# One 512 KB transfer for the first four row tiles, and a new order for the first 200 places of a hand-kept task list

## The chip, the cores and the metric

The kernel runs on one core of one Trainium2 chip. Its time is the device time of one execution in microseconds (us). Three timed runs of the kernel before gave 194.25, 195.13 and 196.08 us; the median, 195.13 us, is what the changed kernel is compared with.

Five engines run side by side, each with its own queue that is worked off in order: PE (matrix products and transposes), DVE and ACT (element-wise work and copies out of PSUM, the memory that PE writes), POOL (small vector work) and SP (which here only issues transfers). An engine that comes to an instruction whose input is not ready waits, and everything behind it on that queue waits too.

## The reference

The input rows are normalized, and two branches run over them. Branch A is a gated long convolution: a four-tap convolution of k, times v, then a convolution over all 2048 positions by FFT, times the rows. Branch B is a gated feed-forward product. They are joined at the end.

```python
x = A_q                                        # 1 x 2048 x 512
xn = _layernorm(x)
k_shift = sum over t of k_pad[:, t:t+S] * shift_k[:, ks-1-t]     # 4 taps
kv = k_shift * v
y = irfft(rfft(kv, 2S) * rfft(ssm_k, 2S))[:S] + kv * ssm_D       # long convolution
s = xn * y
h = gelu(xn @ w_gate) * (xn @ w_up)            # 512 x 1792 weights
g = silu(h @ w_down)                           # 1792 x 512 weights
return x + s * g
```

## The kernel before, in words

The 2048 rows are 16 tiles X of 128 rows, worked in four groups q of four tiles. For each group: statistics of each tile on DVE (line 821 and 822, `ln`), the reciprocal root on POOL (831 and 832), the normalized tile XN on DVE (835), four PE transposes of each tile (854, `xn_transpose`), copied out of PSUM into xnT (609). Then come 14 units m (`unit`): gate and up products (called at line 1117 through 618) of xnT with a 128-column piece of Wg and Wu, gelu of the gate on ACT (1128 or 1137), the product with the up part on DVE (1130 or 1140) into HT. Units 0 and 1 of group 0 are cut into halves a and b of two row tiles each, so that half a needs only tiles 0 and 1. The weights lie in four chunks; chunk 0 serves units 0 and 1, chunk 1 units 2 to 5. Last in each group are the down products with Wd.

The long convolution is done as a two-stage transform by matrix products. Its filter ssm_k is loaded as Hn0 to Hn3 (512 KB each). Hn0 and Hn1 are transposed by PE as f32 pairs (878, `h_transpose`), copied to HTr, and multiplied by the table F1 (`half1`, called "filter halves" here; each is two 128x256 products). Filter half "6/0" is the one of HTr tile 6 and transpose block 0; block 0 comes from Hn0, block 1 from Hn1. HTr holds eight tiles; the transposes of one block come in two lots of four, one for tiles 0 to 3 and one for tiles 4 to 7.

Eleven products of zeros (`warm_up`) run on PE before any data is there.

What sets the order: the program first makes a list of tasks, numbered in the order in which they are added; each issues one or several instructions. `SEQ` names all of them in the order in which they are emitted, so it fixes the order on each engine's queue; a "b" behind a number puts a copy on DVE that would else be on ACT. Waits between engines follow from the data and the buffers. `Sched.run` walks through `SEQ` with estimated durations (`LOAD_NS`, `LANDS`, and so on); these estimates choose only which of several free buffers a task takes, above all which of the eight PSUM banks. All loads named in `ORDER` are issued from the SP queue, in the order that they have in `SEQ`: in the kernel before the first two tiles of X, Hn0, the next two tiles, Hn1, chunk 0 of Wg and Wu, X1 (tiles 4 to 7), chunk 1 of Wg, and so on.

Of the kernel before, what the change touches and what calls it, by code (L numbers as in the profile page):

```python
# [22 lines left out]
LAST = [(0, 384), (384, 512)]  # L23
TURN = 8192
N_WARM = 11
ORDER = "x02 h0 h1 x22 w0 w1 h2 h3 D0 w2 s0 k0 v0 x1 w3 k1 v1 d0 d1 k2 v2 k3 v3 x2 x3"
SEQ = (
# [22 lines left out]
)  # L50
NF_BANKS = 4
ISSUE = 470.0
LOAD_NS = {("x0_", 262144): 1400.0, ("x0_", 131072): 450.0, 262144: 900.0, 524288: 1350.0, ("x", 524288): 2100.0, ("h", 524288): 1300.0, ("wg", 524288): 1550.0, ("wu", 524288): 1450.0, 917504: 2620.0, ("sk", 524288): 1500.0, 344064: 1250.0, 46080: 350.0, 3072: 100.0, 1024: 200.0}
W_XT, W_SW, W_BK, W_BH, W_ZI, W_BI, W_ZK, W_MI, W_G1 = 1665000, 600000, 555000, 703000, 333000, 640000, 490000, 740000, 222000
NC_PAIRS = 4
SMALL = 1.15 * 262144
# [235 lines left out]
class Sched:  # L292
# [8 lines left out]
    FIRST = {"loads": 1050.0, "SP": 30500.0}  # L301
    DRAIN = 121.0
    EARLY, TAKEN, SHARED, WAIT = (0.0, 1.0), 1400.0, 46000.0, 3300.0
    LANDS = (4350.0, 5590.0, 7100.0, 8420.0, 9350.0, 10200.0, 11500.0)

    def __init__(self):
        self.tasks = []
# [37 lines left out]
    def run(self):  # L345
        free = dict(self.FIRST)
        pipe = 0.0
        n_loads = 0
        order = []
        pmode = 0  # L350
        for name in SEQ.split():
            t = self.tasks[int(name.rstrip("b"))]
            eng, dur = t.opts[name[-1] == "b"]
            base = 0.0
            for d in t.deps:
                base = max(base, d.end if eng == d.eng == "PE" else d.end + d.lat + (self.SEM if not d.nbytes or eng != "PE" else 400.0 if d.eng == "loads" else self.HEDGE))
            for b in t.w:
                if b.pool is not None and b.slot is None:
                    f, b.slot = b.pool.find()
                    b.pool.take(b.slot)  # L360
                    base = max(base, f + self.SEM)
            t.start, t.eng = max(base, free.get(eng, 800.0)), eng
            free[eng] = t.end = t.start + dur + (self.DRAIN if eng == "PE" and t.mode != pmode else 0.0)
            pmode = t.mode if eng == "PE" else pmode
            if eng == "loads":
                free[eng] = t.start + dur * (self.EARLY[1] if t.start < self.EARLY[0] else 1.0)
                if n_loads < len(self.LANDS):
                    free[eng] = self.LANDS[n_loads] - self.LOAD_LAT
                n_loads += 1
                t.end = free[eng] + self.LOAD_LAT  # L370
            elif t.nbytes:
                en = t.end
                if en < self.SHARED:
                    free["loads"] += self.TAKEN
                pipe = max(pipe, en + self.DMA_LAT / 2) + t.nbytes / (self.SHARE_BW if en < self.SHARED else self.DMA_BW)
                t.end = pipe + self.DMA_LAT / 2 + (self.WAIT if en < self.SHARED else 0.0)
            for b in set(t.r + t.w):
                b.left -= 1
                b.last_end = max(b.last_end, t.end + t.lat)
                if b.left == 0 and b.pool is not None:  # L380
                    b.pool.release(b.slot, b.last_end)
            order.append(t)
        assert sorted(t.n for t in order) == list(range(len(self.tasks)))
        return order
# [14 lines left out]
def build_kernel(nc, A_q, A_k, A_v, A_shift_k, A_ssm_k, A_ssm_D, B_w_gate, B_w_up, B_w_down, out):  # L399
    with ExitStack() as es0:  # L400
# [107 lines left out]
        def dsem(name):  # L508
            return DSem(nc.alloc_semaphore(name), name)
# [79 lines left out]
        def dma(eng, out_ap, in_ap, sem, r, w):  # L589
            trk.dma(eng, lambda e: e.dma_start(out=out_ap, in_=in_ap), sem, r=r, w=w)  # L590
# [3 lines left out]
        def load(name, out_ap, in_ap, w_res, w_buf, nbytes, ring="SP", r=(), rb=()):  # L594
            sem = dsem("d_" + name)
            ns = LOAD_NS.get((name.rstrip("0123456789"), nbytes)) or LOAD_NS[nbytes]
            last_load[0] = S.add([("loads", ns)], lambda e: dma(ring, out_ap, in_ap, sem, r, w_res), r=rb, w=w_buf, nbytes=nbytes)
# [211 lines left out]

        for what in ORDER.split():  # L810
            if what[0] in "xa" and len(what) == 3:
# [475 lines left out]
```

## Time and profile before

| | |
|---|---|
| three timed runs | 194.25, 195.13, 196.08 us |
| profiled execution, first to last instruction (span) | 193.3 us |
| median of the timed runs less this span | 1.8 us |
| PE busy | 188.6 us, 98% |
| DVE busy | 160.0 us, 83% |
| ACT busy | 125.4 us, 65% |
| granted TensorE clock, mean | 1.000 |

The page gives the span of the profiled execution, and no time of its own for what lies around it (start and finish); the difference of 1.8 us from the timed median stands for that.

In a timeline row the first number is the start in us, the second the length of the merged stretch, then the engine, the line, the operation, what it writes and reads, and how many instructions are merged. PE instructions overlap, so a stretch's length holds a tail that lies under the next row: the pace of PE is read from start to start. In a row of transfers the last number is the time from the issue to the landing.

### The profile page before, as it was taken

Reading aid. Unit: us, or ns where it says so; the run is one execution under the profiler, and the core shown is the slowest. Engines: PE = TensorE matmul, PEld = TensorE weight load, DVE = VectorE, ACT = ScalarE, POOL = GpSimd, SP = SyncE. Lnnn points to the kernel's source line nnn. Section 1 sums busy time; section 2 is a strip of 40 time slices with the busy share of each in tenths; the row PEclk is TensorE's granted clock in tenths of the full one; section 3 lists DMA queues with packets and bytes.
Section 4 is the critical chain, followed back from the end, with each engine's and each line's share of the span. In section 5 each row is a group of like instructions: output and inputs, shape, how many; then the busy total and the mean of one; then the engine's idle time right before and its main releaser. Section 6 shows DMA issues by size and latency. Waiting matters only on the chain.

```text
span 193.3 us, 3502 instructions
## 1 busy us (share of the span) xinstructions
PE 188.6 (98%) x1377; PEld 85.6 (44%) x1377; DVE 160.0 (83%) x245; ACT 125.4 (65%) x170; POOL 13.9 (7%) x32
## 2 busy tenths in 40 slices
PE   7899999999999999999999999999999999999993
PEld 2685544444444444443434433433444334444452
DVE  6699789998999995877888789878897863588993
ACT  6787999969885987868548766856577431232121
POOL 5412420000000000020300000000000000000000
PEclk9999999999999999999999999999999999999999
DMA  5999999999999679999999991984805345939333
GB/s 175 311 307 349 377 400 347 157 249 372 375 374 354 196 264 259 390 323 305 218 285 230 338 320 59 288 276 147 264 10 195 106 140 153 389 112 353 132 139 136
DMA packets 45958, 49.19 MB, mean 254 GB/s; under 512 B 12787, under 2 KB 39671, under 8 KB 45942
## 3 DMA queue, kind: packets, MB, share of 16 engines
q1 hardware_dynamic: 37366, 42.67, 70.1%
q10 hardware_dynamic: 8576, 6.29, 10.3%
q8 instruction: 11, 0.18, 0.4%
q14 instruction: 5, 0.04, 0.1%
HBM read 27.39 MB, written 14.68 MB: 218 GB/s over the span
## 4 chain that ended last, share of the span: by engine, by line
PE 93%; DMA 4%; SPq 1%; DVE 1%; ACT 0%; issue 0%
PE psall L618 86%; PE psall L1028 5%; DMA Hn<-in_A_ssm_k_dram 4%; PE psall L854 1%; SPq L590 1%; PE psall L878 1%; DVE G L1175 0%; DVE G L1174 0%; ACT G L1172 0%
## 5 line engine op out<-in xcount | busy, mean ns | idle before, releaser
L618 PE MATMUL psall<-xnT,Wu 128*128 128x512 bf16 (+1 forms) x232 | 55.8, 372 | 0.0
L618 PE MATMUL psall<-xnT,Wg 128*128 128x512 bf16 (+1 forms) x232 | 55.3, 372 | 0.0
L618 PE MATMUL psall<-Wd,HT 128*128 128x512 bf16 (+2 forms) x238 | 52.0, 367 | 0.0
L1140 DVE TENSOR_TENSOR HT<-psall,GE 128x512 bf16<-128x512 f32 x54 | 36.7, 685 | 15.8 <-PE psall L618 15.4
L1137 ACT ACTIVATE GE<-psall 128x512 bf16<-128x512 f32 x54 | 31.7, 601 | 13.1 <-PE psall L618 12.9
L618 PEld LDWEIGHTS psall<-Wd,HT 128*128 128x128 bf16 x238 | 22.4, 98 | 25.9 <-issue 1.1
L618 PEld LDWEIGHTS psall<-xnT,Wg 128*128 128x128 bf16 x232 | 21.9, 98 | 25.4 <-issue 1.3
L618 PEld LDWEIGHTS psall<-xnT,Wu 128*128 128x128 bf16 x232 | 21.6, 98 | 25.9 <-issue 3.5
L609 ACT ACTIVATE X<-psall 128x1024 bf16<-128x1024 f32 (+1 forms) x18 | 15.1, 843 | 3.3 <-DMA ZH<-X 1.9
L609 ACT ACTIVATE HS<-psall 128x1024 bf16<-128x1024 f32 x14 | 13.7, 1022 | 4.4 <-PE psall L1028 4.4
L1164 ACT ACTIVATE G<-psall 128x512 bf16<-128x512 f32 x12 | 7.0, 598 | 12.9 <-PE psall L618 12.4
L1011 DVE TENSOR_TENSOR KAC<-KAC,KTM 128x2048 bf16<-128x2048 bf16 x12 | 14.6, 1217 | 0.1
L1009 DVE TENSOR_TENSOR KTM<-KK,SKB 128x2048 bf16<-128x2048 bf16 x12 | 14.6, 1217 | 0.0
L609 ACT ACTIVATE BO<-psall 128x1024 bf16<-128x1024 f32 x9 | 9.1, 1022 | 8.2 <-PE psall L1028 7.7
L609 ACT ACTIVATE KB<-psall 128x1024 bf16<-128x1024 f32 x11 | 11.0, 1021 | 3.6 <-PE psall L1028 3.6
L609 ACT ACTIVATE AST<-psall 128x1024 bf16<-128x1024 f32 x12 | 12.4, 1033 | 0.7 <-PE psall L618 0.5
L612 DVE CAST BO<-psall 128x1024 bf16<-128x1024 f32 x7 | 8.5, 1224 | 3.7 <-PE psall L1028 3.7
L821 DVE BATCH_NORM_STATS2 stats<-X 128x6 f32<-128x512 bf16 x16 | 10.3, 675 | 1.1 <-DMA X<-in_A_q_dram 1.1
L1172 ACT ACTIVATE G<-psall 128x512 bf16<-128x512 f32 (+2 forms) x5 | 2.6, 512 | 13.1 <-PE psall L618 13.1
L1091 DVE TENSOR_TENSOR HW<-KB,HW 128x1024 bf16<-128x1024 bf16 x16 | 10.9, 682 | 0.0
L1091 DVE TENSOR_TENSOR HS<-KB,HS 128x1024 bf16<-128x1024 bf16 x16 | 10.8, 682 | 0.0
L1166 DVE SCALAR_TENSOR_TENSOR G<-G,psall 128x512 bf16<-128x512 bf16 x12 | 7.8, 680 | 2.0 <-ACT G L1164 2.0
(83 smaller groups left out, 175.6 us busy)
## 6 DMA issues: line engine op xcount, KB each, us to landing
BH<-ZH SPq DMA_DIRECT2D x8, 512.0 KB, 6.1
HW<-HS SPq DMA_DIRECT2D x16, 256.0 KB, 3.2
BK<-ZK SPq DMA_DIRECT2D x8, 512.0 KB, 5.1
ZI<-BO ACTq DMA_DIRECT2D x16, 256.0 KB, 2.8
BI<-ZI SPq DMA_DIRECT2D x8, 512.0 KB, 4.2
ZK<-AST SPq DMA_DIRECT2D x6, 512.0 KB, 4.1
Hn<-in_A_ssm_k_dram SPq DMA_DIRECT2D x4, 512.0 KB, 8.4
KK<-in_A_k_dram SPq DMA_DIRECT2D x4, 512.0 KB, 8.6
```

The source lines that it names most:

```text
L609: return h.activation(o, i, ACTF.Copy, scale=scale)
L612: return h.tensor_copy(o, i)
L618: return h.matmul(o, lhsT=l, rhs=r, start=st, stop=sp)
L821: t_stats[t] = op([("DVE", 670.0)], lambda e, h, t=t: h.bn_stats(stats[:, t, :], X[:, t, :]), r=[bX[q][t % 4]], w=[bst[t]], rr=[R_X[t]], w ...
L1009: op([("DVE", dur)], lambda e, h, j=j, m=m: h.tensor_tensor(KTM[:, m.slot, :, :], kk(j), sk(j), ALU.mult), r=need + [bSKB[j], a], w=[m], r ...
L1011: op([("DVE", dur)], lambda e, h, m=m: h.tensor_tensor(KAC[:, a.slot, :, :], KAC[:, a.slot, :, :], KTM[:, m.slot, :, :], ALU.add), r=[m], ...
L1028: trk.op("PE", lambda h: h.matmul(ps(s, i)[b, :], lhsT=wt(col)[a, :], rhs=data(col)[a, :], start=n < 16, stop=n >= len(todo) - 16, tile_po ...
L1091: return hd.tensor_tensor(o, flat(KB, kb[h]), o, ALU.mult)
L1137: op([("ACT", act(512))], lambda e, h: h.activation(GE[:, g.slot, :], bank(pg), ACTF.Gelu_apprx_tanh), r=[pg], w=[g], rr=lambda: R_bank(pg ...
L1140: op([("DVE", dve(512, 1))], lambda e, h: h.tensor_tensor(HT[:, q % 2, m, :], bank(pu), GE[:, g.slot, :], ALU.mult), r=[pu, g], w=[bHT[q][m]],
L1164: op([("ACT", act(n))], lambda e, h, g=g, pc=pc: h.activation(g, pc(), ACTF.Tanh, scale=0.5), r=[p], w=[bt], rr=lambda p=p: R_bank(p), ww= ...
L1166: op([("DVE", dve(512, 1))], lambda e, h, g=g, pc=pc: h.scalar_tensor_tensor(out=g, in0=g, scalar=1.0, in1=pc(), op0=ALU.add, op1=ALU.mult ...
```

## The change

The first four tiles of X come in one transfer of 512 KB (128 partitions of 4 KB) in place of two of 256 KB (2 KB per partition): `x04` stands in `ORDER` for `x02` and `x22`. There is one task fewer, so every number above 20 falls by one in the new `SEQ`. The first 200 places of `SEQ` are new; from there on both lists are the same but for that shift. The loads keep their order on the SP queue, the second piece of X left out. The planner's table of landing times counts bytes in place of loads.

Three copies change engine: xnT of tiles 0 and 1 goes from ACT to DVE, the second HTr lot of block 1 from DVE to ACT. On PE each of the first 53 tasks after the warm-up is the same in both lists, in another order; from the 54th on the two queues are equal. The first of them, by name (old numbers in brackets):

| | PE queue before | PE queue after |
|---|---|---|
| 1, 2 | Hn0 transposes, two lots (50, 49) | Hn0 transposes (49, 50) |
| 3, 4 | xn tile 0 (82), filter half 7/0 (117) | Hn1 transposes (54, 53) |
| 5, 6 | xn tile 1 (83), filter half 5/0 (107) | filter half 6/0 (112), xn tile 0 (82) |
| 7, 8 | filter half 6/0 (112), Hn1 transposes (54) | filter half 5/0 (107), xn tile 1 (83) |
| 9, 10 | Hn1 transposes (53), gate 0a (369) | filter half 4/0 (102), xn tile 2 (84) |
| 11, 12 | filter half 5/1 (109), xn tile 2 (84) | filter half 5/1 (109), xn tile 3 (85) |
| 13, 14 | up 0a (370), xn tile 3 (85) | up 1a (378), gate 1a (377) |
| 15, 16 | up 1a (378), gate 1a (377) | gate 0a (369), gate 0b (373) |
| 17, 18 | gate 0b (373), gate 1b (381) | gate 1b (381), up 0a (370) |
| 19 to 21 | up 0b (374), up 1b (382), filter half 7/1 (119) | **gate 3 (389)**, filter half 4/1, up 1b |
| 22 | **gate 3 (389)** | filter half 7/0 |

Gate 3 is the first product that needs chunk 1 of Wg.

On DVE the old order takes the statistics of tiles 0 and 1, then XN of tiles 0 and 1, then the same for 2 and 3. The new one takes all four statistics first, then XN 0, 1 and 2, the copy of xnT 0, XN 3, the copy of xnT 1. On ACT the first copies are, after: HTr of block 0 (52) and of block 1 (56), filter halves 5/0 and 4/0 (108, 103), xnT 2 and xnT 3 (88, 89); then the gelus.

```diff
-ORDER = "x02 h0 h1 x22 w0 w1 h2 h3 D0 w2 s0 k0 v0 x1 w3 k1 v1 d0 d1 k2 v2 k3 v3 x2 x3"
+ORDER = "x04 h0 h1 w0 w1 h2 h3 D0 w2 s0 k0 v0 x1 w3 k1 v1 d0 d1 k2 v2 k3 v3 x2 x3"
 SEQ = (
-    "17 18 0 3 1 2 4 8 5 7 11 20 6 9 50 12 65 66 67 73 19 68 75 74 49 10 76 13 52 21 82 22 86 117 83 69 107 70 71 112 54 72 87 77 56b 78 53 369 "
-    "51 108 36 79 371 109 84 88 80 370 15 85 372 23 31 89 110 378 377 113 27 373 379 381 383 375 14 453 455 457 380 24 458 374 459 25 454 118 382 "
...
+    "0 3 17 2 1 18 19 11 8 9 10 4 12 64 66 65 5 7 48 67 6 72 74 68 69 70 73 13 49 51 53 55 52 76 111 71 20 21 35 22 81 106 75 82 77 107 30 26 78 "
+    "23 85b 101 102 83 87 108 79 84 88 86b 377 376 378 14 458 454 24 456 368 379 372 370 380 374 369 371 388 112 109 31 27 29 382 50 459 452 32 "
...
 )
-LOAD_NS = {("x0_", 262144): 1400.0, ("x0_", 131072): 450.0, ...
+LOAD_NS = {("x0_", 524288): 1400.0, ("x0_", 131072): 450.0, ...
...
-    LANDS = (4350.0, 5590.0, 7100.0, 8420.0, 9350.0, 10200.0, 11500.0)
+    LANDS = ((0.0, 2650.0), (524288.0, 4050.0), (1048576.0, 5450.0), (1572864.0, 6850.0), (1835008.0, 7720.0), (2097152.0, 8590.0), (2621440.0, 10590.0), (3145728.0, 12390.0))
...
-        n_loads = 0
+        n_loads = 0.0
...
-                if n_loads < len(self.LANDS):
-                    free[eng] = self.LANDS[n_loads] - self.LOAD_LAT
-                n_loads += 1
+                n_loads += t.nbytes
+                for (b0, t0), (b1, t1) in zip(self.LANDS, self.LANDS[1:]):
+                    if b0 < n_loads <= b1:
+                        free[eng] = t0 + (t1 - t0) * (n_loads - b0) / (b1 - b0) - self.LOAD_LAT
```

More of the change, by code (lines that the diff above doesn't have):

```diff
@@ L52 @@
 ISSUE = 470.0
-LOAD_NS = {("x0_", 262144): 1400.0, ("x0_", 131072): 450.0, 262144: 900.0, 524288: 1350.0, ("x", 524288): 2100.0, ("h", 524288): 1300.0, ("wg", 524288): 1550.0, ("wu", 524288): 1450.0, 917504: 2620.0, ("sk", 524288): 1500.0, 344064: 1250.0, 46080: 350.0, 3072: 100.0, 1024: 200.0}
+LOAD_NS = {("x0_", 524288): 1400.0, ("x0_", 131072): 450.0, 262144: 900.0, 524288: 1350.0, ("x", 524288): 2100.0, ("h", 524288): 1300.0, ("wg", 524288): 1550.0, ("wu", 524288): 1450.0, 917504: 2620.0, ("sk", 524288): 1500.0, 344064: 1250.0, 46080: 350.0, 3072: 100.0, 1024: 200.0}
 W_XT, W_SW, W_BK, W_BH, W_ZI, W_BI, W_ZK, W_MI, W_G1 = 1665000, 600000, 555000, 703000, 333000, 640000, 490000, 740000, 222000
```

40 rows, old and new, of the table SEQ are left out of this document.

## The prediction

> **What bounds the kernel now.** I read the page first (span and chain by engine), then the chain of waits in order of time, then the waits of PE alone, then the timeline of PE over the first 15 us.
>
> ```profile
> span 193.3 us, 3502 instructions
> PE 93%; DMA 4%; SPq 1%; DVE 1%; ACT 0%; issue 0%
> ```
>
> ```profile
> 2.12 7.16 DMA Hn<-in_A_ssm_k_dram
> ...
> 30.27 51.16 PE psall L618 x238
> ...
> 189.55 0.02 issue
> ```
>
> The chain leaves the loads at 9.3 us and is PE until 189.55. That alone doesn't say that PE never waits in between; its own waits from 6 to 189 us do (waiter, what was waited for, total, times, longest):
>
> ```profile
> PE psall L878 <- DMA Hn<-in_A_ssm_k_dram: 0.5, 1, 0.5
> PE psall L618 <- ACT HTr L609: 0.2, 1, 0.2
> ```
>
> Both fall into the first 11 us; the same question from 11 us on has an empty answer. So PE has a fixed amount of work, and the end moves by just as much as the idle time of PE changes. The change reorders PE's work and adds none. In 51.16 us the chain holds 238 products, 0.215 us each: PE's full pace. All that can be won is what PE lost in this stretch:
>
> ```profile
> 0.97 4.87 PE L618 MATMUL psall<-AST 128*128 128x512 bf16 x11 [0.97 <-DVE AST L671]
> 5.64 1.71 PE L878 MATMUL psall<-ident,Hn 128*128 128x128 f32 x8
> 7.18 0.39 PE L854 MATMUL psall<-ident,XN 128*128 128x128 bf16 x4
> 7.82 0.39 PE L618 MATMUL psall<-HTr,F 128*128 128x256 bf16 x2 [0.25 <-ACT HTr L609]
> 8.04 0.39 PE L854 MATMUL psall<-ident,XN 128*128 128x128 bf16 x4
> 8.27 0.60 PE L618 MATMUL psall<-HTr,F 128*128 128x256 bf16 x4
> 9.32 1.16 PE L878 MATMUL psall<-ident,Hn 128*128 128x128 f32 x8 [0.46 <-DMA Hn<-in_A_ssm_k_dram]
> 10.32 0.60 PE L618 MATMUL psall<-xnT,Wg 128*128 128x256 bf16 x4
> 10.82 0.39 PE L618 MATMUL psall<-HTr,F 128*128 128x256 bf16 x2
> 11.23 0.38 PE L854 MATMUL psall<-ident,XN 128*128 128x128 bf16 x4
> 11.45 0.60 PE L618 MATMUL psall<-xnT,Wu 128*128 128x256 bf16 x4
> ...
> 14.96 0.59 PE L618 MATMUL psall<-xnT,Wg 128*128 128x512 bf16 x2
> ```
>
> Prices, from start to start: two 128x256 products 7.82 to 8.04, 0.22, so four are 0.44; four bf16 transposes 11.23 to 11.45, 0.22; eight f32 transposes 9.32 to 10.32, 1.00 (0.125 each), but 5.64 to 7.18, 1.54 (0.19 each) the first time. The warm-up ran at 4.67 us for eleven, 0.42 each against 0.215 later: the transposes at 7.18 are as long (0.39) as their like at 8.04, so until about 7.0 PE works at half pace, though the mean granted clock in the table above is 1.000. Gaps: 7.18 + 0.22 = 7.40 to 7.82, 0.42; 8.27 + 0.44 = 8.71 to 9.32, 0.61; 10.32 + 0.44 = 10.76 to 10.82, 0.06; 10.82 + 0.22 = 11.04 to 11.23, 0.19. Together 1.28 us; with the 0.5 us that half pace costs the first transposes, 1.8 us is the most that this change could win.
>
> **Part one: the transfers.** Issues on the SP queue, and each one's time to landing:
>
> ```profile
> 0.72 0.40 SPq L590 DMA_DIRECT2D X<-in_A_q_dram  x1
> 1.18 0.42 SPq L590 DMA_DIRECT2D Hn<-in_A_ssm_k_dram  x1
> 1.64 0.43 SPq L590 DMA_DIRECT2D X<-in_A_q_dram  x1
> 2.12 0.44 SPq L590 DMA_DIRECT2D Hn<-in_A_ssm_k_dram  x1
> 3.08 0.70 SPq L590 DMA_DIRECT2D Wu<-in_B_w_up_dram  x1
> 3.83 0.55 SPq L590 DMA_DIRECT2D X<-in_A_q_dram  x1
> 4.42 0.64 SPq L590 DMA_DIRECT2D Wg<-in_B_w_gate_dram  x1
> ```
>
> ```profile
> X<-in_A_q_dram SPq DMA_DIRECT2D x1, 256.0 KB, 3.3
> Hn<-in_A_ssm_k_dram SPq DMA_DIRECT2D x1, 512.0 KB, 4.2
> X<-in_A_q_dram SPq DMA_DIRECT2D x1, 256.0 KB, 6.3
> Hn<-in_A_ssm_k_dram SPq DMA_DIRECT2D x1, 512.0 KB, 7.2
> Wu<-in_B_w_up_dram SPq DMA_DIRECT2D x1, 256.0 KB, 7.9
> X<-in_A_q_dram SPq DMA_DIRECT2D x1, 512.0 KB, 8.6
> Wg<-in_B_w_gate_dram SPq DMA_DIRECT2D x1, 512.0 KB, 10.4
> ```
>
> Issue plus time gives landings: first X piece 4.0, Hn0 5.4, second X piece 7.9, Hn1 9.3, chunk 0 of Wu 11.0, X1 12.4, chunk 1 of Wg 14.8. The steps tell what each added: Hn0 1.4 us for 512 KB, the second X piece 2.5 us for half as much, Hn1 again 1.4. At Hn's pace 256 KB are 0.7, so the second piece cost 1.8 us more than its bytes. The saved issue on SP (0.43) is hidden: the issues run 5 to 7 us ahead of the landings.
>
> What becomes of the 1.8 us? If it belongs to the short piece, it goes, and Hn1 lands at 7.5, chunk 1 at 13.0. If it would come in any case (a few slow transfer engines), nothing goes, and Hn1 stays at 9.3, chunk 1 at 14.8. The nearest row is X1: the same tensor with the same strides, in 512 KB like the new transfer. It took 1.4 us behind chunk 0 of Wu, Hn's pace. So I take the first end. Then four tiles land at 4.0 + 0.7 = 4.7, Hn0 at 6.1, Hn1 at 7.5.
>
> **Part two: PE's new queue.** Durations on the other engines:
>
> ```profile
> L821 DVE BATCH_NORM_STATS2 stats<-X 128x6 f32<-128x512 bf16 x8 | 5.2, 676 | 1.1 <-DMA X<-in_A_q_dram 1.1
> L835 DVE TENSOR_SCALAR XN<-X,mv 128x512 bf16<-128x512 bf16 x8 | 3.1, 405 | 0.7 <-POOL mv L832 0.7
> L609 ACT ACTIVATE HTr<-psall 128x1024 bf16<-128x1024 bf16 x3 | 3.1, 1029 | 1.2 <-PE psall L878 1.2
> L609 ACT ACTIVATE xnT<-psall 128x512 bf16<-128x512 bf16 x4 | 2.4, 596 | 0.6 <-PE psall L854 0.5
> L822 DVE BATCH_NORM_AGGREGATE mv<-stats 128x2 f32<-128x6 f32 x8 | 1.2, 171 | 0.1
> L612 DVE COPY HTr<-psall 128x1024 bf16<-128x1024 bf16 x1 | 0.7, 691 | 0.5 <-PE psall L878 0.5
> ```
>
> DVE: four statistics and three aggregates from 4.7 take 4 x 0.68 + 3 x 0.17 = 3.2, to 7.9; XN 0 to 8.35, the last aggregate, XN 1 to 8.95, XN 2 to 9.35; the copy of xnT 0 is not in the trace in this form, I take 0.42 (between half of the 0.69 of a copy twice as wide and ACT's 0.60), to 9.8; XN 3 to 10.2; xnT 1 to 10.6. POOL's roots are ready before each.
>
> PE: the Hn0 transposes wait from 5.64 to 6.1, run at half pace to 7.0 and end at 7.4. Hn1 has landed at 7.5; eight transposes to 8.4. The filter half 6/0 needs HTr (ACT 7.6 to 8.65), so 8.7 to 8.9. Then xn 0, filter half 5/0, xn 1, filter half 4/0, xn 2, filter half 5/1, 0.22 each, to 10.2: each finds its XN ready, and the second HTr copy ends at 9.7. xn 3 waits for XN 3, to 10.5. Up 1a waits for xnT 1, 10.65; with gate 1a and gate 0a to 12.0. Gate 0b needs xnT 2 and 3 from ACT: behind HTr (9.7) stand two copies of filter halves, as wide as xnT's (0.6 each), and these two, 9.7 + 2.4 = 12.1. Gate 0b, gate 1b and up 0a end at 13.4. Gate 3 starts there, chunk 1 being there since 13.0.
>
> In the old kernel gate 3 started at 14.96, but with more done ahead of it: the two filter halves 7 (0.44) and up 0b and 1b (0.88), less filter half 4/0 (0.22): 1.10 us. So 14.96 - 1.10 = 13.86 is the break-even; 13.4 wins 0.46. Counted the other way, PE's gaps are 0.46 + 0.1 + 0.3 + 0.1 + 0.15 + 0.1 = 1.2 in place of 1.28, and half pace from 6.1 to 7.0 costs 0.3 in place of 0.5: 0.3 won. I take 0.35.
>
> From 13.4 on I carry no new wait: DVE and ACT have their early work behind them at least as soon, and later weights come no later. The sum: 193.3 - 0.35 = 193.0 us of span, and 195.1 - 0.35 = 194.8 in the timed runs.
>
> [...] Half pace ended here at about 7.0 us, after 6 us of unbroken PE work from 0.97; the idle 0.61 us before 9.32 was followed by transposes at 0.125, near full pace. [...]
>
> **The rivals.**
>
> A, the loads don't come sooner (the other side: slower). Place: Hn1's transposes, third in the new queue, with all xn and filter work behind them. For it: nothing in the trace says what held the second piece up, and a lag of some transfer engines would stay. Against: the X1 row. PE idles from 7.2 to 9.3, everything up to gate 3 follows from 9.32 (transposes 1.0, eight pieces of 0.22, six of 0.44: 5.4) to 14.7, and gate 3 starts with its weights at 14.9 as before, 1.1 us of work behind. 195.1 + 1.1 = 196.2. It turns from gain to loss where chunk 1 lands after 13.8, less than 1.0 us sooner than now.
>
> B, the half pace lasts longer. In the trace it took 6 us of unbroken PE work, 0.97 to 7.0, to end it. The gap from 5.64 to 6.1 is new and lies in that stretch. If the count begins anew at 6.1, half pace holds to 12.1: sixteen transposes at 0.19 end at 9.2 instead of 8.4, and the eight pieces behind them, 0.44 each, at 12.4 instead of 10.5. That is 1.9 late; the waits for xnT 1 and xnT 3 (0.25) are then gone. 194.8 + 1.7 = 196.5. Against it: the gap is short, and 0.61 us before 9.32 did not bring the half pace back. [...]
>
> C, DVE holds PSUM banks. In the new order the products HT of units 0 and 1 stand behind three statistics of X1's tiles and a table product, and later the first tap product of the convolution,
>
> ```profile
> 23.32 1.42 DVE L1005 TENSOR_TENSOR KAC<-KK,SKB 128x2048 bf16<-128x2048 bf16 x1
> ```
>
> which waits for its load until about 23.3, stands ahead of HT of unit 4. PE's eight banks are then freed later; at worst PE loses that 1.4 us: 196.2. Against it: the old order has this product on DVE at the same time, between HT products of other units, and no PE wait came of it.
>
> D, nothing: the gaps only move, 195.1. It lies in the forecast's own range.
>
> **Chances and range.** Forecast (from the most that can be won, 1.8, to break-even) 0.57, A 0.23, B 0.08, C 0.07, two of them together (about 197.3) 0.05. Three runs of the kernel before lie from 0.5% below to 0.5% above the median, so under 1% (2 us) can't be told from no change. A gain of 2 us is more than PE idles; only a lucky set of runs shows it: 0.03. A loss of over 2 us needs two rivals together, or one with unlucky runs: 0.07. Within 1%: 0.90. The range: below, all 1.28 us of gaps gone, 193.8; above, A, B and C (196.2 to 196.5) with 0.1 for the runs, 196.6.
>
> **What would show it.** Right: Hn1 lands by about 7.5 and gate 3 (the first Wg products of 128x512) starts near 13.4; PE has no wait after it. Rival A: Hn1 near 9 and a PE wait of about 2 us on it. B: the bf16 transposes after Hn1's at 0.11 each in place of 0.055. C: PE waits on DVE between 14 and 32 us. The forecast is wrong if the four tiles land after 5.5, or if PE waits after 14 us for any reason.

## The result, and the profile after

Six timed runs of the changed kernel gave a median of 201.01 us (199.22 to 202.77), six of the kernel before on the same chip 194.6 us (194.25 to 196.08). The ratio, without the run of 202.77 us, which is over 1.5% above the fastest, is 1.0302, with a 95% interval of 1.027 to 1.0333: 3% slower, where no change was forecast. The profiled execution took 201.02 us, with a span of

```profile
span 199.2 us, 3504 instructions
```

and that is 5.9 us more than the 193.3 of before. The loads of the early part first: the issues on the SP queue, then each one's time to landing (last number, in us).

```profile
0.72 0.40 SPq L591 DMA_DIRECT2D X<-in_A_q_dram  x1
1.18 0.89 SPq L591 DMA_DIRECT2D Hn<-in_A_ssm_k_dram  x2
4.52 0.44 SPq L591 DMA_DIRECT2D Wg<-in_B_w_gate_dram  x1
```

```profile
X<-in_A_q_dram SPq DMA_DIRECT2D x1, 512.0 KB, 4.5
Hn<-in_A_ssm_k_dram SPq DMA_DIRECT2D x1, 512.0 KB, 5.3
Hn<-in_A_ssm_k_dram SPq DMA_DIRECT2D x1, 512.0 KB, 6.3
Wg<-in_B_w_gate_dram SPq DMA_DIRECT2D x1, 512.0 KB, 8.5
```

The four tiles land at 5.2, Hn0 at 6.5, Hn1 (the second of the two issues, at 1.6) at 7.9, chunk 1 of Wg at 13.0. PE's timeline (start, length; the bracket holds the idle time before and what ended it):

```profile
6.65 2.44 PE L879 MATMUL psall<-ident,Hn 128*128 128x128 f32 x16 [1.16 <-DMA Hn<-in_A_ssm_k_dram]
8.93 0.38 PE L619 MATMUL psall<-HTr,F 128*128 128x256 bf16 x2
...
13.72 1.03 PE L619 MATMUL psall<-xnT,Wg 128*128 128x512 bf16 x4
```

PE waits longer for Hn0 than forecast, has smaller waits behind it, and gate 3 starts at 13.72. Up to there the kernel is 0.14 ahead of the profile of before, whose break-even was 13.86. All of the 5.9 us are lost later. PE's waits from 12 us on (waiter, what was waited for, total, times, longest), for which the kernel before had an empty answer:

```profile
PE psall L619 <- ACT X L610: 3.2, 1, 3.2
PE psall L619 <- ACT GE L1138: 0.6, 1, 0.6
```

The same stretch in PE's timeline, with the pace before and after each gap:

```profile
35.85 1.03 PE L619 MATMUL psall<-xnT,Wg 128*128 128x512 bf16 x4
36.88 1.04 PE L619 MATMUL psall<-xnT,Wu 128*128 128x512 bf16 x4
...
38.62 0.59 PE L619 MATMUL psall<-HTr,F 128*128 128x512 bf16 x2
39.84 1.04 PE L619 MATMUL psall<-xnT,Wg 128*128 128x512 bf16 x4 [0.63 <-ACT GE L1138]
...
51.07 1.03 PE L619 MATMUL psall<-xnT,Wg 128*128 128x512 bf16 x4
55.27 0.61 PE L619 MATMUL psall<-HTD,F 128*128 128x512 bf16 x2 [3.17 <-ACT X L610]
...
59.99 1.03 PE L619 MATMUL psall<-xnT,Wg 128*128 128x512 bf16 x4
```

At 0.2165 a product (eight take 1.73, from 49.34 to 51.07), four are 0.87 and two 0.43. So PE idles 36.88 - 36.72 = 0.16, then 39.84 - 39.05 = 0.79, then 55.27 - 51.94 = 3.33 us. From 55.27 to 59.99 it does 14 products, worth 3.03 us, in 4.72: 1.69 us more are lost to a slow pace. Together 5.97, less the 0.14 of the early part: 5.83 of the 5.9 us. The slow pace is the clock; the stretches (length, PE, PEld, DVE, ACT, POOL busy, then the granted clock PEclk, DMA share and GB/s) show it granted at a half for 3.4 us behind the long gap:

```profile
52.79:56.20 3.41, 0.93 (x5) 0.46 (x6) 3.41 (x5) 2.01 (x3) 0.00 (x0) 1.00 1.48 343
56.22:59.62 3.40, 3.40 (x10) 1.22 (x9) 2.32 (x4) 2.34 (x3) 0.00 (x0) 0.50 0.80 223
59.64:63.00 3.36, 3.36 (x17) 1.47 (x16) 2.67 (x4) 2.92 (x4) 0.00 (x0) 1.00 1.05 396
```

This half pace is not in every execution of the changed kernel: the mean granted clock is 0.983 to 0.991 in four of the six timed runs, and 0.998 and 0.999 in the two of 199.22 and 199.51 us.

What PE waited for stands in the chain of waits (start, length, what):

```profile
46.38 7.73 DMA ZH<-X
...
54.19 1.03 ACT X L610
55.27 32.08 PE psall L619 x140
```

A store from a tile of X to ZH is issued at 46.38 and lands at 54.11; a copy on ACT into the same place waits for it; PE needs the PSUM bank that this copy empties. The timelines of ACT before and after, of that store's issue and that copy:

```profile
45.04 0.37 ACTq L590 DMA_DIRECT2D ZH<-X  x1
49.15 1.02 ACT L609 ACTIVATE X<-psall 128x1024 bf16<-128x1024 f32 x1
```

```profile
46.38 0.37 ACTq L591 DMA_DIRECT2D ZH<-X  x1
54.19 1.94 ACT L610 ACTIVATE X<-psall 128x1024 bf16<-128x1024 f32 x2 [3.87 <-DMA ZH<-X]
```

Before, the store issued at 45.04 took 7.2 us too, to 52.2, and yet the copy began at 49.15: it did not need that store. The answer is in how the program gives out buffers. Eight rows of the filter's transform (rows 4 to 7 are copied as two filter halves each) are gathered in four quarters of X, at tiles 8, 10, 12 and 14, then stored to ZH. Each row takes a free quarter in the order in which the rows' first copies stand in `SEQ`. In the old list the first four are rows 5, 6, 7, 4 (copies 108, 113, 118, 103); in the new one 5, 4, 6, 7, since the copy of filter half 4/0 now stands ahead of that of 6/0. So row 6 moves from tile 10 to tile 12. Its store is the last of the eight in both lists (the one of 45.04 and 46.38). A later stage (J) puts its first row into tile 12, in both lists. Before, tile 12 held row 7 and then row 2, whose store was issued 9 us sooner, at 36.14; after, it holds row 6.

The second difference is on ACT's copies HP and the SP queue. HP has two halves, HP0 and HP1. Into each go a copy from Hn2 and one from Hn3, and a transpose by DMA then brings the half into HTD. The four copies and the two transposes, with their first and last start, before and after:

```profile
L609 ACT ACTIVATE HP<-Hn x4: 2081/2090/2117, 18.9 to 33.8; 128x1024 bf16<-128x1024 bf16 x4
L899 SPq DMA_TRANSPOSE HTD<-HP x2: 2322/2722/3122, 32.1 to 35.9; - x2
```

```profile
L610 ACT ACTIVATE HP<-Hn x4: 2078/2116/2151, 26.5 to 37.1; 128x1024 bf16<-128x1024 bf16 x4
L900 SPq DMA_TRANSPOSE HTD<-HP x2: 2044/2148/2252, 33.0 to 39.3; - x2
```

The new list has all four HP copies of 2.1 us in one 13 us stretch of ACT, the last ending at 39.3 in place of 35.9. The second transpose, of HP1, waits for it at the head of the SP queue, and the loads behind it wait too. The first of these in each kernel:

```profile
38.30 1.51 SPq L590 DMA_DIRECT2D V<-in_A_v_dram  x1
```

```profile
41.62 0.67 SPq L591 DMA_DIRECT2D V<-in_A_v_dram  x1
```

So there are two suspects. **Theory S**: the buffer, which puts the J copy behind row 6's store. **Theory H**: the late HP copies, which take ACT at 36 to 39 us (the 0.95 us of small gaps) and set back the SP queue by 3.3 us, with the stores and transposes that follow.

### The profile page after: what moved, and what is told of

It reads as the page before. It is cut to its first block, busy times and chain, and to the rows that moved or that the text cites. A ratio compares the mean times of both kernels' runs of the same rounds, so it can differ in the third digit from the quotient of the medians.

```text
span 199.2 us, 3504 instructions
## 1 busy us (share of the span) xinstructions
PE 190.0 (95%) x1377; PEld 85.3 (43%) x1377; DVE 160.6 (81%) x246; ACT 125.7 (63%) x169; POOL 15.6 (8%) x32
## 4 chain that ended last, share of the span: by engine, by line
PE 85%; DMA 6%; ACT 3%; POOL 2%; DVE 1%; issue 1%; ACTq 0%
PE psall L619 79%; PE psall L1029 5%; DMA ZH<-X 4%; DMA X<-in_A_q_dram 2%; POOL mv L833 1%; ACT GE L1138 1%; ACT TFA L730 1%; PE psall L855 1%; DVE stats L822 1%; ACT X L610 1%; POOL mv L832 0%; ACT TFB L730 0%; ACT xnT L610 0%; DVE G L1176 0%; DVE G L1175 0%
## 5 line engine op out<-in xcount | busy, mean ns | idle before, releaser
L619 PE MATMUL psall<-xnT,Wg 128*128 128x512 bf16 (+1 forms) x232 | 56.3, 376 | 0.6 <-ACT GE L1138 0.6
L619 PE MATMUL psall<-xnT,Wu 128*128 128x512 bf16 (+1 forms) x232 | 56.4, 374 | 0.0
L619 PEld LDWEIGHTS psall<-xnT,Wg 128*128 128x128 bf16 x232 | 22.2, 99 | 26.3 <-issue 2.4
L610 ACT ACTIVATE X<-psall 128x1024 bf16<-128x1024 f32 (+1 forms) x18 | 14.8, 844 | 6.2 <-DMA ZH<-X 3.9
```

The source lines that it names most:

```text
L610: return h.activation(o, i, ACTF.Copy, scale=scale)
L619: return h.matmul(o, lhsT=l, rhs=r, start=st, stop=sp)
```

## The experiments

Numbers of `SEQ` in the diffs are those of the kernel that is edited; 58 and 59 of the new list are 59 and 60 of the old one: the two copies into HP1, the first from Hn2, the second from Hn3.

### e1: the first copy into HP1 early

The new kernel, with copy 58 behind unit 4's gelu. It starts at 22.2 us there; in the kernel before it was the first of the four, at 18.9.

```diff
-"... 147 394 393 395 ..."
+"... 147 394 58 393 395 ..."
...
-"... 420 467 58 413 ..."
+"... 420 467 413 ..."
```

> The kernel after, with one entry of its list moved: the first HP1 copy (from Hn2, 2.1 us on ACT, task 59 in old numbers) goes from behind xn tile 2 of group 1 to behind the gelu of unit 4, where ACT idles in the run of after (20 to 26 us). Theory H (the two HP1 copies end at 39.3 instead of 35.9 on ACT; the second HTD transpose waits for them at the head of the SP queue and holds back the five loads V2, KK3, Wd0, V1 and Wd1 by 3.3 us; the store of ZH at 46.4 then lands only at 54.1, and ACT and PE wait for it): the HP1 copies end about 2 us sooner or more, the PE waits after 36 us (0.95 and 3.3 us, and 1.3 us of half pace behind them) are gone or nearly, time 194.3 to 195.5. Rival R (the new first stretch as a whole - the transfer, the row-tile order - and the HP copies are only a sign of it): 199 or more.

Measured: 198.5 us, ratio 1.0201 (1.014 to 1.0262), between the two theories. 2.5 us came back, not 6. The gaps at 36 to 40 us are gone, but the last HP copy still ends at 38.0, and the load behind the transposes is no sooner:

```profile
42.07 0.97 SPq L591 DMA_DIRECT2D V<-in_A_v_dram  x1
```

PE still waits at 51 to 55 us, 1.80 and 0.92 us, and again at half pace behind it. One copy is not the cause; H in the narrow form that I had then fell.

### e2: the kernel before, with that copy late

```diff
-"... 393 16 59 463 ..."
+"... 393 16 463 ..."
...
-"... 158 93 60 62 ..."
+"... 158 93 59 60 62 ..."
```

> The kernel before, with the same copy moved the other way: the first HP1 copy goes from its early place (18.9 us in the run of before) to right ahead of the second one. Theory H: HP1 ends some 2 us later, near 38; the loads behind the second HTD transpose are issued some 2 us later; a PE wait of 1 to 4 us between 36 and 58 us comes, time 196 to 199. Rival R: the old first stretch is untouched, no wait, 194.6 within 0.5.

Measured: 195.97 us, ratio 1.0068 (1.0044 to 1.0091), just under the 196 to 199 of theory H. The last copy now ends at 37.4 in place of 35.9; this brings the wait for the gelu, but no more:

```profile
37.93 1.04 PE L618 MATMUL psall<-xnT,Wg 128*128 128x512 bf16 x4 [1.11 <-ACT GE L1137]
```

This kernel has the early part of the kernel before, word for word, in a second execution. Its timeline and its transfers:

```profile
13.84 1.03 PE L618 MATMUL psall<-xnT,Wg 128*128 128x512 bf16 x4
```

```profile
Hn<-in_A_ssm_k_dram SPq DMA_DIRECT2D x1, 512.0 KB, 4.0
X<-in_A_q_dram SPq DMA_DIRECT2D x1, 256.0 KB, 4.9
Hn<-in_A_ssm_k_dram SPq DMA_DIRECT2D x1, 512.0 KB, 5.8
```

Issued at 1.18, 1.64 and 2.11, these land at 5.2, 6.5 and 7.9: here the second piece of X adds 1.3 us, not 2.5, and gate 3 starts at 13.84, not 14.96.

### e3: the one transfer alone, with the old list

```diff
-ORDER = "x02 h0 h1 x22 w0 w1 ..."
+ORDER = "x04 h0 h1 w0 w1 ..."
```

(the list as before, renumbered without the second load)

> The transfer alone: the first four tiles in one transfer as in after, but the whole list of before (the second piece's entry left out). Theory H: the transfer is not what costs; HP1 ends at 36 as before and no PE wait follows after 12 us. Hn1 lands near 7.9 instead of 9.3, the four tiles near 5.2 instead of 4.0 and 7.9; PE's gaps before 12 us stay near 1.3, time 194.0 to 195.5. Rival R in the form that the transfer costs: 197 or more.

Measured: 195.05 us, ratio 1.0026 (0.9995 to 1.0057). The transfer is not the cause of the 3%. It brings no gain either: gate 3 starts 0.96 us later than in e2, with Hn0 at 6.5 in place of 5.2.

```profile
14.80 1.03 PE L619 MATMUL psall<-xnT,Wg 128*128 128x512 bf16 x4
```

### e4: the new kernel, with the second transpose behind three loads

The transpose leaves the head of the SP queue; the copies stay late.

```diff
-"... 417 423 61 497 ..."
+"... 417 423 497 ..."
...
-"... 97 419 40 93 89 ..."
+"... 97 419 40 61 93 89 ..."
```

> The kernel after, with the second HTD transpose moved on the SP queue from ahead of the loads V2, KK3 and Wd0 to behind them; ACT, DVE and PE queues as in after. Theory H (the blocked loads are the link): the three loads are issued near 33.5 instead of 41.6, the ZH store lands in about 4 us, the 3.3 us PE wait and the half pace behind it are gone; the 0.95 us of waits between 36 and 39.8, which are ACT's own lateness, stay: 195.2 to 196.2. Rival R2 (the loads are beside the point; ACT's lateness or the late second HTD itself makes the wait): 199 to 202.

Measured: 199.0 us, ratio 1.0196 (1.0131 to 1.0262); missed by 3 us. The loads do go out early, but the store takes as long as before (SP's timeline, then the chain):

```profile
35.92 1.00 SPq L591 DMA_DIRECT2D V<-in_A_v_dram  x1
```

```profile
47.23 6.89 DMA ZH<-X
```

So it is not the late loads that make the store slow: row 6's store takes 6.9 to 8.0 us in every profile in which it is issued late (44 to 47 us), before included. The 2.0 us that came back are mostly the half pace, which no run of e4 has behind this wait (mean granted clock 0.999 and 1.0): against the runs of the changed kernel without it (199.22 and 199.51) it is 0.4. What matters is who waits for it, and that led to the buffers.

### e5: the new kernel, with row 6 out of tile 12

```diff
-        ast = {"H": [quarter(X, j) for j in (8, 10, 12, 14)], ...
+        ast = {"H": [quarter(X, j) for j in (12, 10, 8, 14)], ...
```

Row 6 gets tile 8, and tile 12 goes to rows that are stored sooner (5, then 1).

> The kernel after, its list untouched; only the places of the four H buffers in X are exchanged (tile pairs 12, 10, 8, 14 in place of 8, 10, 12, 14), so that the tile of filter row 6, whose ZH store goes out last on ACT's queue (46.4 us in the run of after), no longer lies where the first J tile is written. Theory S (the new order of the first copies gives filter row 6 the buffer X 12-13, which the J tile must then wait for; in the kernel before it was X 10-11): ACT's 3.9 us wait on the store, PE's 3.3 us wait and the 1.3 us of half pace behind it are gone, while the late HP copies and the 0.95 us of PE waits between 36 and 40 us stay: 195.2 to 196.5. Theory H (it was the late loads): the wait stays, 199 or more.

Measured: 199.75 us, ratio 1.0281 (1.0243 to 1.0319); missed by 3 us. The wait of 3.3 us at 52 us is gone with its half pace, as theory S says, but a new one of 2.6 us comes 9 us later, behind another store:

```profile
55.88 6.23 DMA ZH<-X
```

```profile
63.27 0.60 PE L619 MATMUL psall<-V,F 128*128 128x512 bf16 x2 [2.48 <-ACT X L610]
```

That store is the first of stage J, on the SP queue. It goes out 4.7 us later than in the kernel before (51.21), behind the transposes and loads that H set back. What S says of the place holds, but mending it alone is worth little, since H's delay comes next.

### e6: the new kernel, with row 6's store ahead of the others

```diff
-"... 119 120 469 412 ..."
+"... 119 120 115 469 412 ..."
...
-"... 478 115 161 225 ..."
+"... 478 161 225 ..."
```

> The kernel after with one entry moved: the store of filter row 6 to ZH is issued right behind that of row 7 (near 26 us) and not at 46.4. Buffers as the planner then gives them: X 12-13 passes from row 6 to row 1, whose store went out at 41.2. Theory S: no 3.9 us wait on ACT, 195 to 196.5, like the exchanged buffers. Theory H: 199 or more.

Measured: 198.12 us, ratio 1.0192 (1.0165 to 1.022), 2.9 us better than the changed kernel, and 1.6 above the range of theory S. As in e5 the wait at 52 us is gone and one at 62 us is there, smaller:

```profile
63.53 0.61 PE L619 MATMUL psall<-V,F 128*128 128x512 bf16 x2 [1.58 <-ACT X L610]
```

### e7: the kernel before, with row 6 in tile 12

The converse of e5; nothing else is touched.

```diff
-        ast = {"H": [quarter(X, j) for j in (8, 10, 12, 14)], ...
+        ast = {"H": [quarter(X, j) for j in (8, 12, 10, 14)], ...
```

> The kernel before, its list and transfers untouched; only the places of two H buffers in X are exchanged (8, 12, 10, 14), so that filter row 6 lies in X 12-13 as in after. In the run of before its store went out at 45.0 and took 7.2 us, to 52.2, and the J tile was written there at 49.2. Theory S: ACT waits some 3 us at 49, PE some 2 to 3 us at 51, perhaps with half pace behind: 196.5 to 199.5. Theory H: HP copies and loads are as before, so 194.7 within 0.6.

Measured: 197.55 us, ratio 1.0154 (1.0117 to 1.0191), as theory S said. The three signs of the changed kernel appear in the old one, in the chain, in PE's timeline and in the clock of that stretch:

```profile
44.01 7.14 DMA ZH<-X
```

```profile
52.31 0.89 PE L618 MATMUL psall<-HTD,F 128*128 128x512 bf16 x2 [2.13 <-ACT X L609]
```

```profile
50.00:55.00 5.00, 2.87 (x8) 0.99 (x8) 3.47 (x5) 3.45 (x4) 0.00 (x0) 0.75 1.15 348
```

Two numbers swapped in a list of places cost 3 us (2.4 us in the two of the four runs without half pace, 196.78 and 196.98): that settles S.

### e8: e1 and e6 together

> The kernel after with two entries moved: the first HP1 copy early (as in e1_hp_early) and the store of filter row 6 early. Theories S and H each explain a part: S the 3.3 us wait and the half pace, H the 0.95 us of waits near 37 to 40 and the late loads. If both are right the whole loss is gone: no PE wait over 0.7 us after 14 us, 194.3 to 195.3. If something else of the first 200 places costs, 196 or more.

Measured: 197.43 us, ratio 1.015 (1.0135 to 1.0166); missed by 2 us. The V load still goes out at 42.06, behind the second copy into HP1, which ends at 38.5, and a gap of 1.06 us stays at 60.8. That pointed to both copies into HP1.

### e9: both copies into HP1 early, and the store early

```diff
-"... 392 114 385 147 ..."
+"... 392 114 58 385 147 ..."
...
-"... 95 96 155 420 467 58 413 ..."
+"... 95 96 59 155 420 467 413 ..."
...
-"... 428 59 92 416 ..."
+"... 428 92 416 ..."
```

(and the two edits of e6)

> The kernel after with three entries moved: the first HP1 copy behind the copy of filter half 6/1 (ACT idles there, 20.6 us in the run of after), the second HP1 copy behind the copy of filter row 2, so that HP1 should be done near 36 as in before (39.3 in after, 38.0 in e1_hp_early), and the store of filter row 6 right behind that of row 7. Theory S+H (two separate losses: the buffer that the J tile waits for, and the late HP1 that holds back the loads and with them the J stores behind them on SP): the second HTD transpose is issued near 36.5, the loads by 38.5, no ACT wait on a ZH store over 1 us, no PE wait over 0.7 us: 194.2 to 195.5. If something else in the first 200 places costs: 196.5 or more.

Measured: 195.47 us, ratio 1.0058 (1.0038 to 1.0079); 5.5 us came back. SP is through with the transposes at 38.4, as in the kernel before (38.3), and PE has no wait after 12 us:

```profile
33.01 5.38 SPq L900 DMA_TRANSPOSE HTD<-HP  x2
38.43 1.58 SPq L591 DMA_DIRECT2D V<-in_A_v_dram  x1
```

The first store of stage J goes out at 52.14. In e5, e6 and e8 it went at 55.88, 56.39 and 54.38, with a PE wait each time.

### e10: the two copies into HP1 alone

As e9, with the store where the new list has it.

> As e9_hp_both_zh6, but the store of filter row 6 stays at its late place, so the J tile still waits for it. Theory S+H: HP1 and loads are on time, and the buffer wait alone is left, as in e7_before_layout (a PE wait of about 2.3 us near 50 us and up to 1.9 us of half pace): 196.5 to 198.5. If the buffer matters only when the loads are late: 194.2 to 195.5.

Measured: 197.54 us, ratio 1.0154 (1.0132 to 1.0177), as expected. The store is again what PE waits for, at 45.13 to 52.37:

```profile
45.13 7.24 DMA ZH<-X
```

Four kernels now make a square: neither edit 201.0, the copies alone 197.5, the store alone 198.1, both 195.5. The copies give back 3.5 and 2.6 us, the store 2.9 and 2.1. That each seems worth less where the other is mended comes from the half pace, which of the four only the first has. Counted from its two runs without it (199.22 and 199.51), the copies give back 1.8 and the store 1.2, less than the 2.6 and 2.1 where the other is mended.

### e11: the new list with the old two transfers

```diff
-ORDER = "x04 h0 h1 w0 w1 ..."
+ORDER = "x02 h0 h1 x22 w0 w1 ..."
```

(and the second load back in the list)

> The new list alone: the queues of PE, DVE, ACT and POOL exactly as in after, but the first four tiles in two transfers, the second behind Hn0, as in before. Both theories: the loss is the list's. The late waits come as in after, and Hn1 lands near 9.3 instead of 7.9, so gate 3 starts near 14.8 instead of 13.7: 200.5 to 203. If the one transfer were part of the loss: below 200.

Measured: 200.68 us, ratio 1.0289 (1.0249 to 1.033): the time as expected, so the list carries the loss. But Hn1 was expected at 9.3, and landed at 2.11 + 5.9 = 8.0:

```profile
X<-in_A_q_dram SPq DMA_DIRECT2D x1, 256.0 KB, 5.0
Hn<-in_A_ssm_k_dram SPq DMA_DIRECT2D x1, 512.0 KB, 5.9
```

Gate 3 was expected near 14.8, and started at 13.46. With e2 and e7 (8.0) this is the third execution in which the two transfers bring Hn1 when the one transfer does.

### e12: e9 with two transfers

> The list of e9 (both copies of HP and the store of row 6 put back in time), with the first row tiles in two transfers of 256 KB as in the kernel before. Two theories on what is left of e9's 0.9 us over the kernel before (195.47 against 194.56). Theory L, the new early order: in the run of two transfers under the new list gate 3 started at 13.46, in that of one transfer at 13.72, and in the undisturbed run of the old list (HP late) at 13.84 with 1.10 us more done ahead of it; so two transfers give 0.26 back and the order keeps 0.7: 195.0 to 195.4. Theory T, the transfer: the whole remainder goes, 194.5 to 194.9. Both: Hn0 near 5.3, Hn1 near 8.0, gate 3 near 13.5, no PE wait after 12 us.

Measured: 195.45 us, ratio 1.0066 (1.0033 to 1.0099), just above what theory L said, and far from T. PE's timeline has gate 3 at

```profile
13.35 1.03 PE L619 MATMUL psall<-xnT,Wg 128*128 128x512 bf16 x4
```

which is 0.4 sooner than with one transfer; a gap of 0.42 at 36.4 us, ended by a gelu (0.13 in e9), takes most of that back. So what is left in e9 and e12, about 1 us, does not hang on the transfer. It fits the early order: e9's gate 3 starts at 13.74, e2's at 13.84 with 1.10 us more done before it, 1.0 us behind. The order of these 53 tasks was not undone by itself, so this last microsecond is worked out, not shown. None of the twelve kernels is faster than the kernel before.

## Why the prediction was wrong

**What bounds the kernel** was right. PE's lost time explains the change: 5.83 us of 5.9, and in e9, where PE has no wait after 12 us, the time is back within 0.6%.

**Part one, the transfers.** The forecast landings, 4.7, 6.1, 7.5 and 13.0, came out 5.2, 6.5, 7.9 and 13.0. The mis-sized term is the first: I put the second half of the tiles at Hn's pace (0.7 us), and it adds 1.2. The sentence that fails is "the second piece cost 1.8 us more than its bytes". True of that execution, it is not of the piece: in e2, e7, e11 and e12 it adds 1.4, 1.1, 1.3 and 0.7 us to Hn0's landing. In the profile of before, 14 of the 16 transfer engines had done their share of the second piece by 6.39 us, the last two at 7.32 and 7.90; in those four all sixteen had by 6.5 to 6.6. The one transfer thus brings Hn0 0.7 to 1.3 us later than the old two, and Hn1 no sooner than they mostly do (7.9 to 8.1).

**Part two, PE's queue to gate 3.** Forecast 13.4, break-even 13.86, measured 13.72. The gap ahead of Hn0 took 1.16 us in place of 0.46: Hn0 landed 0.4 later, from the same term, and the warm-up was done sooner. I carried half pace to 7.0; the trace of the changed kernel has the full clock from 5.01, and the first eight transposes took 1.0 us, not 1.3. So the step came near by two errors that partly cancel, which is luck. Against the profile of before, 0.14 us was won where I took 0.35. But that profile had the slow landing in it. Measured by e2's gate 3 the break-even is 13.84 - 1.10 = 12.74, and the new early part is 1.0 us behind.

**The step that failed** is "From 13.4 on I carry no new wait: DVE and ACT have their early work behind them at least as soon, and later weights come no later." The runs put 6.0 us in its place. I followed PE's 53 tasks one by one, and the other engines only up to 12 us. Of the 200 new places most lie later. Among them were the four HP copies, which end 3.4 us later, and with them the second transpose and the loads behind it on the SP queue (H: 3.5 us less in e10, which mends only this, 1.8 against the changed kernel's runs without half pace). The other half is no late engine: the new order gave row 6 another buffer (S: 2.9 us less in e6, 1.2 against those runs; 3 us when forced on the old kernel in e7). The prediction followed engines and landings, and not the buffer that a moved task takes.

**The rivals.** A's mechanism did not occur as written, since Hn1 landed at 7.9. Its core, that the loads come no sooner, holds against the usual landing, and its price, 1.1 us, is near what e9 and e12 have left. B did not occur in the profile of the changed kernel (16 transposes in 2.28 us), but did in those of e6 and e4, after gaps of 0.73 and 0.83 us; e4's rows:

```profile
6.67 3.61 PE L879 MATMUL psall<-ident,Hn 128*128 128x128 f32 x16 [0.83 <-DMA Hn<-in_A_ssm_k_dram]
10.12 0.39 PE L619 MATMUL psall<-HTr,F 128*128 128x256 bf16 x2
```

Sixteen in 3.45 us is 0.216 each, and the products behind them, two in 0.22, are at full pace from 10.12 on (in e6 the first two, from 10.02 on, still take 0.33, and the next 0.22 from 10.35): two microseconds sooner than the 12.1 of my count begun anew. Nor is it the gap alone, as B had it: in e9 and e10, after 0.81 and 0.79 us, the first eight transposes make a stretch of 1.13 us, as in the changed kernel; in the profile of before, mostly at half pace, they made one of 1.71. C did not occur in the changed kernel; no wait on DVE stood between 14 and 32 us. The real rival, a late one on ACT and SP, was not on the list, and so "a loss of over 2 us needs two rivals together" was wrong. The closing test was the right one: "if PE waits after 14 us for any reason".

## What to carry to other kernels

When a list of tasks is made anew, follow every moved task to the end of the moved stretch, on every engine and queue, and work out which buffer each one gets: where buffers are given in list order, a swap of two copies decides which later stage waits for which store. Row 6's store took 7.2 us in the kernel before, and PE had no wait from 12 us on; in the changed kernel, where its place was wanted, it took 7.7 and cost PE 3.3 us, and 1.7 more with the clock. And a landing that stands out in one profile should be seen in a second execution before a gain is built on it.

## What the runs showed of the hardware

The wait of 3.33 us on PE cost 1.69 us more in slow pace. The trace of the changed kernel has the full clock from 5.01 to 56.21 us, half to 59.63, then full again: 3.41 us at half. In e1 and e11 the granted clock is 0.66 over 55 to 60 us, in e7 it is 0.75 over 50 to 55 and 0.91 over 55 to 60, which makes 3.4 us at half in each. The length of the wait does not decide whether that comes. In the profile of e5, PE's gap of 2.63 us had the full clock behind it; in that of e7, the gap of 2.28 had half. PE's gaps of over 0.3 us between 50 and 64 us in the profiles (from start to start, as above), and the timed runs:

| kernel | PE's gaps, us | clock behind them in the profile | timed runs with a mean granted clock of 0.991 or less |
|---|---|---|---|
| changed kernel | 3.33 | half | 4 of 6 |
| e11 | 1.26, 1.86 | half | 3 of 4 |
| e1 | 1.80, 0.92 | half | 1 of 4 |
| e5 | 2.63 | full | 2 of 4 |
| e7 | 2.28 | half | 2 of 4 |
| e10 | 0.64, 1.32 | full | 0 of 4 |
| e6 | 1.74 | full | 0 of 4 |
| e4 | 0.67, 1.39 | full | 0 of 4 |
| e8 | 1.06 | full | 0 of 4 |

The five with 2.28 us or more in all show the low clock in some of their executions and not in others, the four with 2.06 or less in none. Why one execution has it and another of the same kernel has not, no run shows. The price of the same wait changes with it: e7 has a mean granted clock of 0.99 and 0.991 at 198.16 and 198.12 us, and of 0.998 and 0.999 at 196.98 and 196.78. No timed run of e4, e6, e8, e9 or e10 is below 0.998. One run of e12 is, 0.991 at 197.04 us; it has no trace, and its cause stays open.

The column of the granted clock does not show the half pace at the start. In the profile of before the record begins with a full clock at 7.00 us, as the prediction read from the pace, and the column says 1.00 for 0 to 5 and for 5 to 7 us too. In e4 the column says 1.00 in the stretch where the transposes ran at 0.216 each:

```profile
8.00:10.00 2.00, 2.00 (x11) 2.00 (x11) 1.41 (x5) 1.34 (x2) 1.83 (x5) 1.00 1.08 380
```
